# Host layout by tiles, merged weight halves and a reordered first stage in a two-branch mixer kernel

## The chip, the core and the metric

The kernel runs on one core of a Trainium2 chip. Five engines work side by side, each through its own queue in order: TensorE (PE; its weight loads are listed as PEld), VectorE (DVE), ScalarE (ACT), GpSimd (POOL) and SyncE (SP), which here issues all DMAs. The metric is the device time of one execution in microseconds (us). A profile shows one execution: its span runs from the first to the last instruction, and the time of that execution is a little longer than its span.

## The reference

One sequence of 2048 tokens with 512 channels. Each token is normalised, and the result goes two ways: a sliding, dilated attention with 32 heads of 16 channels, in which a token looks at itself and at 7 earlier ones at a distance of 2, 4, ... 14; and a two-layer MLP with 1376 hidden units. The branches are multiplied and added to the input.

```python
xn = _layernorm(x, axis=-1)
s = _A_ref(xn, A_wqkv, A_wo)            # attention, see below
g = _silu(_B_ref(xn, B_w1, B_b1, B_w2, B_b2))   # w2 . gelu(w1 . xn + b1) + b2
return x + s * g

# in _A_ref: H = 32, Dh = 16, W, dil = 8, 2
idx = pos[:, None] - off[None, :]       # off = arange(W) * dil, masked where negative
logits = einsum("bhsd,bhswd->bhsw", q, kg) * scale
o = einsum("bhsw,bhswd->bhsd", softmax(logits), vg)
return o.transpose(...).reshape(B, S, D) @ wo
```

## The kernel before

**Tiling.** Token s is p * 16 + i * 2 + c, with p the partition (0 to 127), i one of 8 tiles and c one of 2 parities. With a dilation of 2 the parities never meet in the attention, so the work is cut by c. A tile (c, i) is 128 tokens by 512 channels, 256 KB.

**Numbers in two halves.** Matmuls run in 16 bit. Every weight and every activation is split into a high half (rounded) and a low half (the rest), and a product is three matmuls: high by high, high by low, low by high. Weights are first scaled by a power of two that comes from the sum of their squares: ACT squares and sums (`sumsq`, L339; `prep_q`, L402), PE adds the sums over the partitions with a matrix of fours (`total`, L345), DVE takes the exponent and builds the scales in some four one-column operations (L349 to L369). Then `split` makes the high half on ACT (L376) and the low half on DVE (L377). The q, k and v weights have their own copy of this (L413 and L417).

**Stages.** For parity 0, `ln0` takes groups of tiles: statistics on DVE (L458, L459), the power -1/2 on POOL (L443), the normalised tile on DVE (L484) or ACT (L462), a transpose on PE (L491), high half on ACT (L495), low half on DVE (L496). Group order is tiles 2, 3, (0, 1), (4, 5), (6, 7). The loads ahead of it are the weights of head block 0 in two halves, then tiles 2, 3, (0, 1), (4, 5), (6, 7); behind them w1, head block 1, the rest of w1, w2 (L876 to L908). For parity 1, `ln1` does the same later through transposing DMAs.

The attention has 8 units (c, hb), a parity by a block of 8 heads. `qkv` is 8 tiles of 12 matmuls on PE (L545), and ACT scales them into one of two buffers U (L553); DMAs copy shifted rows for the neighbours (L562). `attention` is nearly all DVE: products with the eight neighbours (L596), sums over 16 channels (L599), softmax, products with the values (L653) and their sum (L648), the two halves of the result (L636 on ACT, L638 on DVE) and a transposing DMA to oT (L641).

The MLP is 44 steps (ch, f): 4 chunks of 512 tokens by 11 blocks of hidden units. `mlp1` does 12 matmuls of 512 columns (L785), gelu on ACT (L798), the high half on ACT (L801), the low half on DVE (L804), or, for the first 8 steps, on PE and ACT (L810, L813). `mlp2` adds the step into 4 PSUM tiles (L826), two steps behind `mlp1`. `mlp1` has two PSUM buffers (`mh`). The output projection is L723 (`wo_first` for parity 0, `wo_last` for parity 1), followed by a multiplication with the gate (L737, L767), the addition of x (L714, L716) and the store (L717).

**Order.** Nothing is ordered by hand. Each operation is registered with an engine, a duration, what it reads and writes and a priority (`Plan.add`); `Plan.issue` simulates the engines, at each step places the operation that can start first (within 0.05 us the one with the lowest priority number), and so fixes the order of every engine's queue. On the chip only the order remains: an operation that is ready still stands behind the one that was placed before it. Important priorities: statistics of `ln0` 0.1, evacuation of `qkv` 0.15, low halves of head block 0 0.135, head block 1 0.7, the sums of w2 0.74, w1 0.75, splits of w2 0.9; attention and `qkv` of later units 1000 and up, the MLP 1000000 and up.

Ring buffers (`Ring`) are given out in the same simulation: `prod` 3 of 8 KB a partition, `f` 7 of 2 KB, `ps` and `mh` 2 PSUM banks each.

Of the kernel before, what the change touches and what calls it, by code (L numbers as in the profile page):

```python
# [8 lines left out]
F32 = mybir.dt.float32  # L9
# [9 lines left out]
P = 128  # L19
# [12 lines left out]
NFB = 7  # L32
LAG = 2
# [4 lines left out]
LOADS = ["q0", (2, 1), (3, 1), (0, 2), (4, 2), (6, 2)]  # L38

ACT_Y = (0, 1, 4, 5)  # L40

# [29 lines left out]
class Plan:  # L71
# [5 lines left out]
    def __init__(self):  # L77
        self.ops, self.writer, self.readers, self.prio = [], {}, {}, 0.0

    def add(self, eng, dur, fn, reads=(), writes=(), prio=None, table=None, nbytes=0,  # L80
# [3 lines left out]

        o = Op()
# [24 lines left out]
        return o  # L110

# [25 lines left out]
    def place(self, o, t):  # L137

        if o.eng == "sp":
            if not o.nbytes:  # L140
                return t
            self.free["sp"] = t + o.issue
            self.dma = max(self.dma, t + o.issue + 0.3) + o.nbytes / o.rate
            end = self.dma + o.tail
            self.landed.append(end)
            return end
# [24 lines left out]
    def issue(self):  # L171
# [6 lines left out]
        while len(order) < len(self.ops):  # L178
            best = None
            for e, cand in engs.items():  # L180
# [13 lines left out]
                if lst:  # L194
                    t0 = min(x[0] for x in lst)
                    t, o = min((x for x in lst if x[0] <= t0 + WINDOW), key=lambda x: (x[1].prio, x[1].n))
                    if best is None or t < best[0]:
                        best = (t, o)
# [26 lines left out]

QUEUE = 8
# [6 lines left out]

PLN = 0.1
WINDOW = 0.05
DVE1 = 1.0417e-3
ACT1 = 0.833e-3


@with_exitstack  # L240
def tile_mixer(ctx, tc, a_x, a_wqkv, a_wo, b_w1, b_b1, b_w2, out):
# [30 lines left out]
    xv = a_x[0].rearrange("(p i c) d -> c p i d", i=NI, c=DIL)  # L272
    ov = out[0].rearrange("(p i c) d -> c p i d", i=NI, c=DIL)
    w1v = b_w1.rearrange("(k p) f -> p k f", p=P)


# [17 lines left out]
    wq = sb.tile([P, NHB, KT, 2, 384], F16, name="wq")  # L294
    w1 = sb.tile([P, KT, 2, F], F16, name="w1")
    w2 = sb.tile([P, NF, 2, D], F16, name="w2")
    wo = sb.tile([P, KT, 2, D], F16, name="wo")
# [6 lines left out]
    gd = dr.tile([DIL, P, NI, D], F32, name="gd")  # L304
# [30 lines left out]
    def sumsq(col, ckey, src, skey, junk, jkey):  # L335

        get = src if callable(src) else lambda: src
        n = get_n(src)
        act(n, lambda: nc.scalar.activation(junk().bitcast(BF16), get(), AF.Square, accum_out=col()),  # L339
            [skey], [ckey, jkey])  # L340

    def total(dst, dkey, cols, n, ckeys, late=False):

        b = (R_ps if late else R_z[0]).new()
        pl.add("pe", 0.3, lambda: nc.tensor.matmul(b.t[:, 0:n], fours, cols()[:, 0:n], start=True,  # L345
                                                   stop=True), ckeys, [b], prio=min(pl.prio, PTOT))
# [26 lines left out]
    def split(hi, lo, src, s, r, w):  # L373
        get = src if callable(src) else lambda: src
        n = get_n(src)
        act(n, lambda: nc.scalar.activation(hi, get(), AF.Identity, scale=s), r, [(w, "hi")])  # L376
# [11 lines left out]


    def load_q(hb):  # L390
        pre = pl.users(stkey[hb])
        for k in range(0, KT, 2):
            dma(P * 3072, lambda k=k: nc.sync.dma_start(stq[hb]()[:, k * 384:(k + 2) * 384],
                                                        a_wqkv[hb, :, k * 384:(k + 2) * 384]),
                [], [("stq", hb, k), ("stq", hb, k + 1)] + stkey[hb], after=pre)

    def prep_q(hb):
        col = R_s.new()
        for k in range(0, KT, 2):
            def go(k=k):  # L400
                src = stq[hb]()[:, k * 384:(k + 2) * 384]
                nc.scalar.activation(wq[:, hb, k:k + 2, 0].bitcast(BF16),  # L402
# [4 lines left out]
        total(lambda: ssq[:, hb:hb + 1], ("ssq", hb), lambda: col.t, 2, [(col, 0), (col, 2)],  # L407
              late=hb > 1)
        h = half_exp(lambda: ssq[:, hb:hb + 1], ("ssq", hb))
        up(qsc[:, hb, 0:1], ("qs", hb), h)  # L410
        for k in range(KT):
            def hi(k=k):
                nc.scalar.activation(wq[:, hb, k, 0], stq[hb]()[:, k * 384:(k + 1) * 384],  # L413
                                     AF.Identity, scale=qsc[:, hb, 0:1])

            def lo(k=k):
                nc.vector.scalar_tensor_tensor(  # L417
                    wq[:, hb, k, 1], stq[hb]()[:, k * 384:(k + 1) * 384], qsc[:, hb, 0:1],
                    wq[:, hb, k, 0], op0=ALU.mult, op1=ALU.subtract)
            r = [("stq", hb, k), ("qs", hb)]  # L420
            act(384, hi, r, [("wqh", hb, k)], holds=stkey[hb])
            dve(384, lo, r + [("wqh", hb, k)], [("wq", hb, k)], holds=stkey[hb], c=0.125,
                prio=0.135 if hb == 0 else None)
        down(qsc[:, hb, 1:2], ("qi", hb), h, 24.0)
# [5 lines left out]
    def factors(n, mv, mk, cdst, ckeys, **k):  # L430
# [11 lines left out]
            mk, [p0b], **k)  # L442
        pool(0.42 + 0.14 * n, lambda: nc.gpsimd.tensor_tensor(  # L443
            rb.t[:, 0:n], p0b.t[:, 0:n], halves[:, 0:n], op=ALU.pow), [p0b], [(rb, 0)], **k)
        dve(n, lambda: nc.vector.tensor_scalar(a0(), V(), EPS, None, op0=ALU.add), mk, [(A, 0)])
        dve(n, lambda: nc.vector.reciprocal(a1(), a0()), [(A, 0)], [(A, 1)])
        dve(n, lambda: nc.vector.tensor_tensor(a1(), a1(), V(), op=ALU.mult), [(A, 1)] + mk, [(A, 1)])
        dve(n, lambda: nc.vector.tensor_scalar(a1(), a1(), EPS, None, op0=ALU.add), [(A, 1)], [(A, 1)])
        dve(n, lambda: nc.vector.scalar_tensor_tensor(rb.t[:, 8:8 + n], mv()[:, 0:n, 0], -1.0,
                                                      rb.t[:, 0:n], op0=ALU.mult, op1=ALU.mult),  # L450
            mk + [(rb, 0)], [(rb, 1)], c=0.125, **k)
        pool(0.42 + 0.14 * n, lambda: nc.gpsimd.tensor_tensor(
            cdst, a1(), halves[:, 8:8 + n], op=ALU.pow), [(A, 1)], ckeys)
        return rb

    def stats(mv, a, key, x, xkey, **k):
# [9 lines left out]
    def ln0(ii, xs, xkeys):  # L466
# [5 lines left out]
        for a in range(n):  # L472
            stats(mv, a, mk[a], xs[a], xkeys[a], **first)
# [633 lines left out]
```

## Time and profile before

| | us |
|---|---|
| median of 3 runs | 425.3 (423.86 to 426.49) |
| the profiled execution: time | 426.52 |
| the profiled execution: span | 424.7 |
| time outside the span | 1.8 |
| granted TensorE clock, mean | 0.992 |

The page gives busy time by engine, the span in 40 slices as digits, the chain of work that ended last, and groups of instructions with count, busy time, mean duration in ns of one, and the engine's idle time before them. A line of the timeline is start, duration, engine, source line, operation, output <- inputs, and in brackets the idle time before it and what ended it; successive alike instructions are merged with a count. DVE's and ACT's instructions overlap a little, so that the mean duration is about 0.1 us over the step from one start to the next.

### The profile page before, as it was taken

To read this page: it belongs to the slowest core of one execution; us is meant where nothing else is said; L and a number is where in the kernel's file an instruction comes from. 1 tells how busy PE (TensorE), PEld (TensorE's weight loads), DVE (VectorE), ACT (ScalarE), POOL (GpSimd) and SP (SyncE) were. 2 spreads that over 40 slices of the span, in tenths; PEclk is the share of its full clock that TensorE was granted. 3 is DMA by queue.
4 is the path that set the end of the run, shared out by engine and by line. 5 is a ranking of instruction groups with operands and counts; after the bars stand their busy time and mean duration, and the time that the engine had idled before them with its cause. 6 is when DMAs were issued, how large, how long until landed. Compare 5 with 4: busy or idle time off the path is not lost.

```text
span 424.7 us, 5503 instructions
## 1 busy us (share of the span) xinstructions
PE 406.7 (96%) x2072; PEld 206.6 (49%) x2072; DVE 396.7 (93%) x434; ACT 217.6 (51%) x340; POOL 97.8 (23%) x87
## 2 busy tenths in 40 slices
PE   0999979999999999999999999999999999999995
PEld 0666524445544654445544654455445544444442
DVE  3998999998999979999999999998999999999966
ACT  4799975845376456744466254125312284226400
POOL 5310202002500382002700360046002610250013
PEclk9999969999999999999999999999999999999999
DMA  8964420003241235742162034022423264005325
GB/s 277 412 245 148 146 79 0 2 7 143 85 101 50 100 87 120 129 109 43 54 180 100 0 88 99 2 74 80 155 98 107 69 161 174 0 2 127 122 49 198
DMA packets 43050, 44.83 MB, mean 106 GB/s; under 512 B 27496, under 2 KB 28064, under 8 KB 42768
## 3 DMA queue, kind: packets, MB, share of 16 engines
q1 hardware_dynamic: 43024, 44.49, 34.7%
q8 instruction: 16, 0.26, 0.3%
q14 instruction: 10, 0.08, 0.1%
HBM read 23.53 MB, written 7.34 MB: 73 GB/s over the span
## 4 chain that ended last, share of the span: by engine, by line
PE 84%; ACT 9%; DVE 3%; DMA 2%; issue 1%; SPq 0%; DVEq 0%
PE z L826 27%; PE mh L785 26%; PE ps L545 22%; PE ps L723 6%; ACT w L376 2%; ACT U L553 2%; DMA prod<-in_A_x_dram 2%; ACT w L339 1%; PE z L723 1%; PE mh L723 1%; DVE U L714 1%; DVE U L767 1%; ACT wq L402 1%; ACT yT L495 1%; DVE bn L458 1%
## 5 line engine op out<-in xcount | busy, mean ns | idle before, releaser
L545 PE MATMUL ps<-wq,yT 128*128 128x384 f16 x768 | 129.3, 328 | 0.0
L785 PE MATMUL mh<-yT,w 128*128 128x512 f16 (+1 forms) x528 | 123.5, 385 | 0.9 <-ACT h L813 0.9
L826 PE MATMUL z<-w,h 128*128 128x512 f16 x480 | 112.0, 379 | 0.0
L545 PEld LDWEIGHTS <-yT 128*128 128x128 f16 x768 | 75.5, 99 | 51.1 <-issue 1.5
L785 PEld LDWEIGHTS <-w 128*128 128x128 f16 (+1 forms) x528 | 53.4, 101 | 65.8 <-issue 6.3
L798 ACT ACTIVATE mh<-mh,b1T,hsc 128x512 f32<-128x512 f32 (+1 forms) x44 | 33.0, 749 | 88.0 <-PE mh L785 87.8
L596 DVE TENSOR_TENSOR prod<-U 128x2048 f32<-128x2048 f32 x32 | 74.1, 2317 | 1.0
L826 PEld LDWEIGHTS <-h 128*128 128x128 f16 x480 | 47.1, 98 | 55.3 <-issue 0.3
L599 DVE TENSOR_REDUCE L<-prod 128x128 f32<-128x2048 f32 x32 | 72.9, 2279 | 0.3
L553 ACT ACTIVATE U<-ps,cs 128x384 f32<-128x384 f32 x64 | 37.2, 581 | 67.4 <-PE ps L545 63.4
L653 DVE TENSOR_TENSOR prod<-L,U 128x2048 f32<-128x2048 f32 x28 | 63.4, 2285 | 0.1
L676 POOL COPY gate<-prod 1x1 f32<-1x1 f32 x21 | 4.4, 208 | 210.7 <-DVE prod L596 204.2
L648 DVE TENSOR_TENSOR prod<-prod,prod 128x2048 f32<-128x2048 f32 x16 | 36.5, 2284 | 0.0
L677 POOL TENSOR_TENSOR prod<-prod 128x1024 f32<-128x1024 f32 x14 | 32.9, 2347 | 0.0
L723 PEld LDWEIGHTS <-oT 128*128 128x128 f16 x192 | 18.8, 98 | 22.4
L801 ACT ACTIVATE h<-mh,hsc 128x512 f16<-128x512 f32 x40 | 27.4, 685 | 0.9
L723 PE MATMUL ps<-wo,oT 128*128 128x512 f16 x120 | 26.9, 379 | 0.0
L804 DVE SCALAR_TENSOR_TENSOR h<-mh,hsc,h 128x512 f16<-128x512 f32 x32 | 23.8, 744 | 2.8 <-ACT h L801 2.8
L607 POOL TENSOR_TENSOR L<-L,misc 1x384 f32<-1x384 f32 x8 | 19.4, 2430 | 20.6 <-DVE L L599 20.6
L677 POOL TENSOR_TENSOR prod<-prod,prod 128x1024 f32<-128x1024 f32 x7 | 16.4, 2344 | 0.0
L798 ACT ACT_TABLE_LOAD x12 | 15.4, 1283 | 0.2
L636 ACT ACTIVATE o<-prod,osc 128x1024 f16<-128x1024 f32 (+1 forms) x9 | 9.4, 1050 | 11.5 <-DVE prod L648 6.2
(144 smaller groups left out, 338.1 us busy)
## 6 DMA issues: line engine op xcount, KB each, us to landing
f<-in_A_x_dram SPq DMA_DIRECT2D x31, 256.0 KB, 3.7
U<-U SPq DMA_DIRECT2D x16, 392.0 KB, 3.7
gd<-f SPq DMA_DIRECT2D x12, 256.0 KB, 2.0
oT<-in_B_w_dram SPq DMA_DIRECT2D x2, 1024.0 KB
yT<-in_B_w_dram SPq DMA_DIRECT2D x2, 1024.0 KB
f<-gd SPq DMA_DIRECT2D x8, 256.0 KB, 3.4
out_dram<-f SPq DMA_DIRECT2D x8, 256.0 KB, 2.0
out_dram<-U SPq DMA_DIRECT2D x8, 256.0 KB, 2.3
```

Of the source, the lines that this page charges most:

```text
L545: nc.tensor.matmul(b.t[:, 0:384], y[:, s, k, o:o + P], wq[:, hb, k, t], start=(n == 0), stop=(n == 11))
L553: act(384, lambda i=i, b=b: nc.scalar.activation(U3[:, i:i + 31:15, :], b.t[:, 0:384].rearrange("p (t e) -> p t e", t=3), AF.Identity, sca ...
L596: dve(2048, lambda p2=p2, g=g: nc.vector.tensor_tensor(p2(), q, slots(Ut, KH, 2 * g), op=ALU.mult), qk + [("kh", ub, 0), ("kh", ub, 1), (" ...
L599: dve(2048, lambda pr=pr, g=g: nc.vector.tensor_reduce(L3()[:, 2 * g:2 * g + 2], pr.t.rearrange("p (r f d) -> p r f d", r=2, d=DH), AX.X, ...
L648: dve(n, lambda: nc.vector.tensor_tensor(d(), a(), b(), op=ALU.add), keys, [dkey])
L653: dve(2048, lambda: nc.vector.tensor_tensor(pr.t.rearrange("p (r f d) -> p r f d", r=2, d=DH), L3()[:, 2 * g:2 * g + 2].rearrange("p r (f ...
L677: nc.gpsimd.tensor_tensor(x.t[:, 0:1024], x.t[:, 0:1024], y(), op=ALU.add)
L723: nc.tensor.matmul(b.t, oT[:, hb, i // 4, s, i % 4], wo[:, hb, t], start=(hb == 0 and n == 0), stop=(hb == NHB - 1 and n == 2))
L785: nc.tensor.matmul(b.t[0:M], w1[:, k, s, f * P:f * P + M], yT[ch][:, t, k], start=(n == 0), stop=(n == 11))
L798: act(512, lambda: nc.scalar.activation(b.t[0:M], b.t[0:M], AF.Gelu_apprx_tanh, bias=b1T[0:M, f:f + 1], scale=hsc[0:M, 1:2]), [b, ("b1T",) ...
L801: act(512, lambda: nc.scalar.activation(hi()[0:M], b.t[0:M], AF.Identity, scale=hsc[0:M, 2:3]), [b], [hk])
L826: nc.tensor.matmul(z.t, hl[s][0:K, t * P:(t + 1) * P], w2[0:K, f, w], start=(f == 0 and n == 0), stop=(f == NF - 1 and n == 2))
```

## The change

On the host x, the result, w1 and the buffer for the gate get new layouts: x and the result as (c, i, p, d), so that a tile is one piece of 256 KB in DRAM and not 128 rows 32 KB apart; w1 as [128, 4 * 1376], so that a part of any width is one run a partition. In the kernel:

- *Merged tensors.* The high halves of wq, w1, w2 and wo each become one block, the low halves another (`[P, 2, KT, F]` for `[P, KT, 2, F]`), so that one instruction can cross rows of weights. w1 is loaded, summed and split in 4 parts of 2048, 2048, 1024 and 384 columns instead of 8 (1024 and 352); w2 and wo in blocks of 1024 columns, head blocks 1 to 3 in blocks of 768.
- *Other engines.* w1's high halves go from ACT to DVE (`W1DVE`). The sums for w2's first eight rows go from DVE statistics (L974 to L981) to two ACT square sums of 2048 columns. The bias of ACT's normalisation is a one-column operation on ACT and no longer one on DVE behind POOL (L449).
- *Order.* Head block 0's weights and the first two x tiles are loaded in turn. Statistics of the pairs of tiles wait until tiles 2 and 3 are normalised (`behind`). Chains of small DVE operations are registered as one (`Plan.fuse`). The low halves of head block 0 get priority 0.45. w1's sums get 0.72, ahead of w2's, and wait for ACT's four normalised tiles (`BEFORE_W1`). The splits of w2 from row 4 on are put among the MLP's steps (`W2LATE`). A gelu of one element loads the table ahead of the first real one (`warm`). 16 matmuls whose result is not used, with the lowest priority, wait for the normalised tile 2 (`WAKE`). The tile order of the first unit is 2, 3, 0, 1, 4, ... The first matmuls of `qkv` and `mlp1` are registered in smaller groups.
- *Planner.* DMAs of the first 7.8 us are planned at 265 GB/s, those of the first loads otherwise at 395 to 400 GB/s with a shorter tail; ties between engines go by priority.

```diff
+W1C = [0, 2048, 4096, 5120, KT * F]
-LOADS = ["q0", (2, 1), (3, 1), (0, 2), (4, 2), (6, 2)]
+LOADS = ["q0", (2, 1), "q2", (3, 1), (0, 2), (4, 2), (6, 2)]
+W1DVE = (0, 1, 2, 3)
+W2P = (0, 2, 4, 6, 8, 9, 10)
+W2LATE = 4
+BEFORE_W1 = (0, 1, 4, 5)
...
+    def fuse(self, eng="dve"):
+        u = self.fused = dict(eng=eng, dur=0.0, fns=[], reads=[], writes=[], port=False, prio=1e12)
+        yield
+        self.fused = None
+        self.add(eng, u["dur"], lambda: [f() for f in u["fns"]], u["reads"], u["writes"],
+                 prio=u["prio"], port=u["port"])
...
-    xv = a_x[0].rearrange("(p i c) d -> c p i d", i=NI, c=DIL)
-    ov = out[0].rearrange("(p i c) d -> c p i d", i=NI, c=DIL)
+    xv, ov = a_x, out
...
-    w1 = sb.tile([P, KT, 2, F], F16, name="w1")
-    w2 = sb.tile([P, NF, 2, D], F16, name="w2")
+    w1 = sb.tile([P, 2, KT, F], F16, name="w1")
+    w2 = sb.tile([P, 2, NF, D], F16, name="w2")
...
+    def split(hi, lo, src, s, r, w, eng="act", n=None):
+        elif eng == "dve":
+            dve(n, lambda: nc.vector.tensor_scalar(hi, get(), s, None, op0=ALU.mult), r, [(w, "hi")], f=0.72)
...
+        behind = [("yd", i) for i in (2, 3) if n > 1]
+        fz = pl.fuse()
+        for a in range(n - 1):
+            stats(mv, a, mk[a], xs[a], [xkeys[a]] + behind)
+        fz.__enter__()
+        stats(mv, n - 1, mk[n - 1], xs[n - 1], [xkeys[n - 1]] + behind)
...
-    IORD = [2, 3, 1, 4, 5, 6, 7, 0]
+    IORD, IORD0 = [2, 3, 1, 4, 5, 6, 7, 0], [2, 3, 0, 1, 4, 5, 6, 7]
...
+    idle = fours.bitcast(BF16)
+    for _ in range(WAKE):
+        b = R_mh.new()
+        pl.add("pe", 0.2, lambda b=b: nc.tensor.matmul(b.t[:, 0:2 * P], idle[:, 0:P], idle, start=True,
+                                                       stop=True), [("yd", 2)], [b], prio=1e9)
...
+    for n in range(4):
+        with prio(PS1):
+            sumsq(lambda n=n: cw1.t[:, n:n + 1], (cw1, n), s1[n], [s1k[n]] + [("y_", i) for i in BEFORE_W1],
+                  lambda n=n: w1f[0][:, W1C[n]:W1C[n + 1]], ("w1h", n), W1C[n + 1] - W1C[n])
...
-            dve(512, lambda h=h, k=k, st=st: nc.vector.bn_stats(
-                st.t[:, 6 * k:6 * k + 6], (s2a, s2b)[h][:, k]), [("s2", h)], [(st, k)], port=False)
+        sumsq(lambda h=h: col5.t[:, h:h + 1], (col5, h), (s2a, s2b)[h].rearrange("p k f -> p (k f)"),
+              [("s2", h), (col5, h)], lambda h=h: w2[:, 0, 4 * h:4 * h + 4].rearrange("p k f -> p (k f)"),
+              ("w2j", h), 2048)
...
+        with prio(PW2 if k < W2LATE else PR_H + 1 + (10 * k - 15) * 1e-6):
+            split(*hl, src, zsc[0:K, 0:1], r, ("w2", k), "pool" if k in W2POOL else "act", n=512 * n)
+    act(1, lambda: nc.scalar.activation(warm, ident[0:1, 0:1], AF.Gelu_apprx_tanh),
+        [("y", 0, i) for i in range(NI)] + [("wq", 1, k) for k in range(KT)], [("warm",)], table="gelu")
...
+    lay["A_x"] = inputs["A_x"].reshape(P, NI, DIL, D).transpose(2, 1, 0, 3)
+    lay["B_w1"] = inputs["B_w1"].reshape(KT, P, F).transpose(1, 0, 2).reshape(P, KT * F)
```

340 lines of the change are left out of this document (188 added, 152 removed).

## The prediction

> **What bounds the kernel now.** I read the page first (busy shares, the clock row, the chain that ended last), then the waits of PE, then the timeline of the first 70 us, then the groups of instructions, then the last 30 us.
>
> ```profile
> span 424.7 us, 5503 instructions
> PE 406.7 (96%) x2072; PEld 206.6 (49%) x2072; DVE 396.7 (93%) x434; ACT 217.6 (51%) x340; POOL 97.8 (23%) x87
> PEclk9999969999999999999999999999999999999999
> PE 84%; ACT 9%; DVE 3%; DMA 2%; issue 1%; SPq 0%; DVEq 0%
> ```
>
> TensorE is busy nearly all the time, VectorE almost as much. The question is therefore where PE does not work at its pace, and how close behind it DVE is. The stretches from 60 to 400 us, summed, answer for the main part:
>
> ```profile
> sum 340.00, PE 340.00 PEld 169.60 DVE 329.10 ACT 164.06 POOL 79.34; mean PE 10.00 PEld 4.99 DVE 9.68 ACT 4.83 POOL 2.33
> ```
>
> PE never stops there, and DVE stops for only 11 us. So the change can win only before 60 us, in the clock dip that the clock row shows in its sixth slice, and in the last few us. PE's own waits are all early:
>
> ```profile
> PE z L345 <- ACT wq L402: 6.3, 1, 6.3
> PE z L491 <- DVE f L484: 4.3, 1, 4.3
> PE mh L810 <- ACT h L801: 2.1, 1, 2.1
> PE mh L785 <- ACT h L813: 0.9, 1, 0.9
> ```
>
> **The start: loads, first tile, first matmuls.**
>
> ```profile
> 9.27 1.29 DVE bn L458 x2
> ```
> ```profile
> 3.94 0.84 ACT L402 ACTIVATE wq<-prod 128x768 bf16<-128x768 f32 x1 [1.94 <-DMA prod<-in_A_wqkv_dram]
> 5.31 0.84 ACT L402 ACTIVATE wq<-prod 128x768 bf16<-128x768 f32 x1 [0.43 <-DMA prod<-in_A_wqkv_dram]
> 5.96 0.70 DVE L458 BATCH_NORM_STATS2 bn<-prod 128x6 f32<-128x512 f32 x1 [4.96 <-DMA prod<-in_A_x_dram]
> 7.90 1.09 POOL L443 TENSOR_TENSOR lw<-lw,halves 128x1 f32<-128x1 f32 x2 [2.96 <-DVE ssq L351]
> 8.38 2.13 ACT L413 ACTIVATE wq<-prod,qsc 128x384 f16<-128x384 f32 x4 [2.13 <-DVE qsc L369]
> 10.53 0.54 DVE L484 TENSOR_SCALAR f<-prod,lw,lw 128x512 f32<-128x512 f32 x1
> 11.22 1.94 PE L491 MATMUL z<-ident,f 128*128 128x128 f32 x8 [4.33 <-DVE f L484]
> 12.98 3.39 PE L545 MATMUL ps<-wq,yT 128*128 128x384 f16 x12
> 17.08 4.06 PE L545 MATMUL ps<-wq,yT 128*128 128x384 f16 x24
> ```
> ```profile
> L440 DVE TENSOR_SCALAR lw<-lw 128x2 f32<-128x2 f32 (+1 forms) x5 | 0.8, 158 | 0.0
> ```
>
> The first normalised tile (10.53) had its power from POOL at 7.90 + 1.09 = 8.99; it stood in DVE's queue behind the statistics of tiles 0 and 1, whose load landed only at 9.27. The change makes those statistics wait for the first two normalised tiles instead, and puts tile 2's load between the two weight halves. That half landed 0.65 us ahead of tile 2 (5.31, 5.96) and 1.37 behind the first (3.94): in turn, I put tile 2 at about 4.85 (3.94 plus 0.65 to 1.2) and the second weight half at 5.96. From there: statistics 0.70, about 0.4 for the three small operations behind them (0.158 each by the last row, now together and overlapping), POOL 0.55 (half of 1.09), so DVE normalises at about 6.6 and PE transposes at 7.2, 4.0 earlier than 11.22. From transposes to first matmuls took 12.98 - 11.22 = 1.76, giving 9.0. The weights come 0.65 later but their four scale operations no longer share DVE's queue with statistics, so the first high half is there near 8.6 and the last, at 2.13/4 each, at 10.2. First matmuls 9.0 to 9.5: 3.5 to 4.0 earlier.
>
> Not all of that lasts. Twelve matmuls took 3.39 at 12.98; 24 took 4.06 at 17.08, so 0.169 each when fast and 0.28 when slow. PE is at a slow pace from 11.22 to about 16.4, 5.2 us, though the clock row shows no dip there. The 16 idle matmuls wait for the same normalised tile as the first transposes, so they cannot begin the waking earlier; they only fill gaps. Waking at 7.2 + 5.2 = 12.4, the matmuls from 9.2 on lose about (12.4 - 9.2)/2 = 1.6, as much as now (3.39 - 12 x 0.169 = 1.4): no gain. By the slow 384-column matmul an idle one of 256 columns costs 0.28 x 256/384, at most 0.2; if all 16 stood ahead of needed ones they would cost 3.2, at the least nothing, since PE has about 1 us of gap behind the first transposes and more until the low weight halves exist. The low halves now have lower priority than all statistics; a PE gap of 0 to 2.5 us is the other unknown. I take 1 us for both together: 3.7 - 1.0 = 2.7 earlier when PE ends the first two head blocks.
>
> The Trainium skill ("TensorE: Matmul & The Clock Gate", What's actually happening) says the full clock comes after about 3.4 us of sustained work and not after a number of matmuls. The trace needed 5.2; by the page's figure the sum would be 0.9 us better, estimated. It speaks against the idle matmuls as such, which the trace bears out: they start no earlier than the work.
>
> **The middle: weights of the MLP, first gelu, clock dip.**
>
> ```profile
> 36.75 0.28 PE L345 MATMUL z<-s,fours 128*128 128x8 f32 x2
> 48.78 5.34 PE L785 MATMUL mh<-yT,w 128*128 128x512 f16 x24
> 56.23 0.38 PE L810 MATMUL mh<-h,dg 128*128 128x512 f16 x1 [2.10 <-ACT h L801]
> 57.47 5.28 PE L785 MATMUL mh<-yT,w 128*128 128x512 f16 x12 [0.87 <-ACT h L813]
> 66.24 2.75 PE L785 MATMUL mh<-yT,w 128*128 128x512 f16 x12
> ```
> ```profile
> 52.70 1.28 ACT L798 ACT_TABLE_LOAD   x1
> 54.00 0.75 ACT L798 ACTIVATE mh<-mh,b1T,hsc 128x512 f32<-128x512 f32 x1
> ```
> ```profile
> L376 ACT ACTIVATE w<-yT,zsc 128x512 f16<-128x512 f32 x8 | 5.3, 722 | 0.0
> L376 ACT ACTIVATE w<-oT,hsc 128x1024 f16<-128x1024 f32 x4 | 4.5, 1153 | 0.0
> L339 ACT ACTIVATE w<-oT 128x1024 bf16<-128x1024 f32 x4 | 4.2, 1058 | 0.0
> L339 ACT ACTIVATE w<-o 128x352 bf16<-128x352 f32 x2 | 1.0, 490 | 0.0
> L339 ACT ACTIVATION_READ_ACCUMULATOR w<-oT 128x1 f32 x4 | 0.8, 203 | 0.0
> L377 DVE SCALAR_TENSOR_TENSOR w<-yT,zsc,w 128x512 f16<-128x512 f32 x8 | 5.8, 744 | 0.0
> L377 DVE SCALAR_TENSOR_TENSOR w<-oT,hsc,w 128x1024 f16<-128x1024 f32 x4 | 4.9, 1274 | 0.0
> L596 DVE TENSOR_TENSOR prod<-U 128x2048 f32<-128x2048 f32 x32 | 74.1, 2317 | 1.0
> L974 DVE BATCH_NORM_STATS2 mx<-yT 128x6 f32<-128x512 f32 x8 | 5.3, 679 | 0.0
> L484 DVE TENSOR_SCALAR f<-prod,lw,lw 128x512 f32<-128x512 f32 x4 | 2.1, 542 | 0.0
> ```
>
> The first MLP block ends at about 48.78 + 2.67 = 51.4, but its gelu starts at 54.00, because ACT is still at weights and then loads a table. PE, with both buffers full, idles, and its next 12 matmuls run at half pace: 5.28 against 2.75 at 66.24, 2.5 us. If ACT is free in time, the correction matmul follows the second block at 48.78 + 5.19 = 53.97 and the third block starts 57.47 - 56.23 = 1.24 later, at 55.2 instead of 57.47: 2.3. With the dip gone, 2.3 + 2.5 = 4.8 us. PE then still idles about 0.9, against 2.1 + 0.9 now, which I take as too short for a dip.
>
> Is ACT free? Against now, ahead of the first gelu: high halves of w1 leave for DVE, 4 x 1.153 and four of 352 columns at the slope of these rows, (1153 - 722)/512 = 0.842 ns a column, so 0.59 each, -7.0; of w2's high halves eight of 0.722 and three of the same width become two of 1.153, the rest comes later, -7.9 + 2.3 (later ACT has room: 164 of 340 us); the w2 sums arrive, two of 2048 columns. A square sum costs (1058 - 490)/672 = 0.845 ns a column plus 0.19, and 0.20 to read it, so 2.13 each, +4.3; eight w1 sums become four, -1.6; a bias operation for four tiles, by the 0.203 row +0.8. In all -9.1. The table load only moves. ACT must be free at 51.4 - 2.7 = 48.7, 5.3 before 54.00: 3.8 us of margin, which also covers the idle time that ACT may get.
>
> Is w1 there? Its four sums now come ahead of w2's, so the total moves from 36.75 to about 32 to 33. Then DVE does high and low halves: high, 5504 columns at (542 - 158)/510 = 0.753 ns plus 4 x 0.158, 4.8 (542 for 512 columns, 158 for 2); low, 5504 at (1274 - 744)/512 = 1.035 ns plus 4 x 0.214, 6.6. That ends near 44.5, at 47 if one product of the attention (2.317) is put in between; PE needs three parts from 46.1 to 48. Tight, but in time. The high halves' bounds: 5504/512 x 0.542 = 5.8 above, the slope alone, 4.1, below; I keep 4.8, since both rows carry it.
>
> So PE arrives 2.7 + 4.8 = 7.5 us earlier: a span of 417.2 if it alone decides.
>
> **DVE and the end.**
>
> ```profile
> 407.93 0.75 DVE L638 SCALAR_TENSOR_TENSOR o<-prod,osc,o 128x512 f16<-128x512 f32 x1 [0.79 <-ACT o L636]
> 420.33 0.75 DVE L767 SCALAR_TENSOR_TENSOR U<-z,osc,U 128x512 f32<-128x512 f32 x1 [1.27 <-PE z L723]
> ```
> ```profile
> DMA to landing us min/median/max: 4.3/4.4/4.4
> ```
>
> The last attention output leaves DVE at 408.68; its transposing DMA lands 4.4 us later (413.1), and 12 matmuls (2.6) and the tail from 420.33 to 424.7 (4.4) remain: 420.1. PE hides that today. Once PE is over 4.6 us earlier, DVE sets the end. DVE's work changes by -5.3 (w2 statistics) and their small followers of about 1, -16 x 0.214 = -3.4 for sixteen merged low halves, +4.8: -4.9. But part of what goes lay ahead of the attention, where DVE may now stand idle until the first head block is complete, and late low halves of w2 move behind the start of the attention. Ends for DVE's gain: 0 and 5.7; I take 3, for the first head block is complete about 3 us earlier. 420.1 - 3 = 417.1, level with PE's 417.2.
>
> Forecast: span 417.2, 7.5 less. The profiled run took 426.52 (1.8 outside its span), 1.2 over the median 425.3; so 425.3 - 7.5 = 417.8. The new layouts of x, output and gate buffer move the same bytes in the same 2 KB rows; only the last store is on the path, so I count nothing for them beyond the order of the first loads.
>
> **The rivals.**
> - DVE gains nothing (idle where the statistics were): span 420.1, time about 420.7. For it: DVE stops only 11 us in 340. Against: it begins attention earlier. 0.14.
> - The middle stall stays: w1 arrives after PE, or ACT after it, so the dip returns. Only 2.7 remains: 422.0, time 422.6. For it: the 1 to 2 us of margin on w1. 0.12.
> - Better: PE keeps all 3.7 of the start; the idle matmuls close the gaps so that the cold loss (1.4) and the 0.9 us idle go too; and tiles laid out in one piece load faster. Today three tiles landed in 9.27 - 5.96 = 3.3 us, 1.1 each, against 0.65 for tile 2; at 0.65 the pair comes 1.4 sooner. 3.7 + 1.4 + 0.9 + 4.8 + 1.4 = 12.2: span 412.5, time 413.1. It needs 7.6 from DVE as well, more than its work shrinks, so half of its 11 us of stops would have to go. 0.18.
> - Slower: DVE takes over. The attention begins no earlier, and the high halves (4.8) and the late low halves of w2 (two of 1.274, three of 0.744: 4.8) all come on top of it: 420.1 + 9.6 = 429.7, time 430. It decides once DVE carries over 4.6 us more behind its first product than now. Against it: the low halves are done ahead today too. 0.06.
>
> **How the numbers follow.** The forecast has 0.50, with its own range 415 to 420. Low 412.5 takes in the better case, high 423 the stall at 422.6; only the slower rival and the far ends stay out. About 1 per cent (4.3 us) can be told from no change, so faster means under 421.0: 0.50 + 0.18 + two thirds of the DVE case 0.10 + a little of the stall 0.02: 0.80. Within: the rest of these two, 0.14, less 0.01 for a stall that grows: 0.13. Slower: 0.06 + 0.01 = 0.07.
>
> **What would show it.** First matmuls with wq near 9 to 9.5; a gelu near 49 with its table loaded before; no sixth-slice dip in the clock row; PE's waits after 20 us under 2 us; in the last 15 us a wait of PE for the last transposing DMA. Wrong if PE waits for w1 near 46, or if DVE's last attention output is not before 408.

## The result and the profile after

The changed kernel takes 428.06 us (median of 8, 427.61 to 430.1), the kernel before 424.47 on the same chip (median of 8, 423.81 to 426.49): a ratio of 1.0081, 95% interval 1.0063 to 1.01. It is slower by 0.8 per cent; 417.8 was predicted, in a range up to 423. The profiled execution took 430.1 (span 428.3), 2.0 above its median, as that of before stood 2.0 above its own (426.52 against 424.47), so the two traces may be set against each other: 3.6 us. (Both were taken in executions with a dip of the clock, which not every execution has; see the section on why the prediction was wrong.)

The page: span, busy shares, the granted clock, the chain that ended last.

```profile
span 428.3 us, 5505 instructions
PE 409.2 (96%) x2098; PEld 208.4 (49%) x2098; DVE 397.6 (93%) x400; ACT 218.7 (51%) x327; POOL 95.8 (22%) x87
PEclk9999989999999999999999999999999999999999
PE 69%; DVE 18%; ACT 4%; issue 3%; DMA 3%; SPq 1%; POOL 0%; DVEq 0%; ACTq 0%
```

DVE's share of the last chain went from 3 to 18 per cent. Its busy time did not fall. The dip in the clock stands at the sixth digit as before, only flatter (8 for 6): the granted clock is 0.50 between 58.0 and 61.2 us, and in the kernel before between 56.6 and 63.2.

**The start.** The timeline of the changed kernel, rows of DVE, PE and ACT:

```profile
6.39 0.55 DVE L559 TENSOR_SCALAR f<-prod,lw,lw 128x512 f32<-128x512 f32 x1
6.99 1.12 PE L566 MATMUL z<-ident,f 128*128 128x128 f32 x4 [1.49 <-DVE f L559]
10.06 0.37 PE L620 MATMUL ps<-wq,yT 128*128 128x384 f16 x1
...
14.69 0.81 ACT L532 ACTIVATE f<-prod,lw 128x512 f32<-128x512 f32 x1
...
18.89 0.68 DVE L523 BATCH_NORM_STATS2 bn<-prod 128x6 f32<-128x512 f32 x1
...
21.20 0.81 ACT L532 ACTIVATE f<-prod,lw 128x512 f32<-128x512 f32 x1
...
49.97 5.34 PE L862 MATMUL mh<-yT,w 128*128 128x512 f16 x24
```

The first tile is normalised 4.1 us earlier (10.53 before), the first matmuls with weights come 2.9 earlier (12.98). But the first tile on ACT is no earlier (14.69; 14.60 before), the statistics of tile 5 come at 18.89, and the next tile on ACT at 21.20 (19.99 before). The first MLP block starts at 49.97 instead of 48.78: the start loses 1.2 us.

**The middle.** First the first split of w2 in the timeline of the kernel before, then the timeline of the changed kernel, with the way of w2's sums to its scale:

```profile
36.50 0.72 ACT L376 ACTIVATE w<-yT,zsc 128x512 f16<-128x512 f32 x1
```
```profile
43.94 0.21 ACT L1068 ACTIVATION_READ_ACCUMULATOR w<-f 97x1 f32 x1
...
44.83 1.28 ACT L1098 ACT_TABLE_LOAD   x1
...
47.24 0.28 PE L394 MATMUL z<-s,fours 128*128 128x5 f32 x2
...
49.72 0.14 DVE L418 TENSOR_SCALAR zsc<-s 128x1 int32<-128x1 int32 x1
...
49.90 1.15 ACT L434 ACTIVATE w<-yT,zsc 128x1024 f16<-128x1024 f32 x1 [1.09 <-DVE zsc L418]
...
51.41 2.18 ACT L434 ACTIVATE w<-yT,zsc 128x1024 f16<-128x1024 f32 x2
53.49 0.74 ACT L879 ACTIVATE mh<-mh,b1T,hsc 128x512 f32<-128x512 f32 x1
54.16 1.14 ACT L434 ACTIVATE w<-yT,zsc 128x1024 f16<-128x1024 f32 x1
55.20 0.68 ACT L882 ACTIVATE h<-mh,hsc 128x512 f16<-128x512 f32 x1
...
57.78 2.60 PE L862 MATMUL mh<-yT,w 128*128 128x512 f16 x6 [1.48 <-ACT h L894]
```

The table is loaded early, as intended. But the last of w2's sums is there only at 44.15, PE adds them up at 47.24, DVE has the scale at 49.86, and ACT, which has waited for it, starts the splits at 49.9, 13.4 us later than before. From there they stand ahead of the first gelu (53.49; 54.00 before) and between it and its high half (55.20). PE's third MLP block starts at 57.78 (57.47 before).

**DVE.** Two windows, before and then after: busy time of PE, PEld, DVE, ACT and POOL.

```profile
25.00:40.00 15.00, 15.00 (x97) 9.27 (x96) 13.88 (x39) 15.00 (x39) 0.38 (x1) 1.00 0.50 162
```
```profile
25.00:40.00 15.00, 14.77 (x95) 9.29 (x96) 7.83 (x20) 15.00 (x26) 0.00 (x0) 1.00 0.42 120
```

DVE, busy 13.88 of these 15 us before, is busy 7.83: what stood there, w2's statistics, is gone, and nothing else is ready. Its first product of the attention comes at 57.54 (37.98 and 56.97 before). The timeline, at PE's one wait after 60 us and in the last us, behind the first row of the last projection in the kernel before:

```profile
411.06 1.46 PE L723 MATMUL ps<-wo,oT 128*128 128x512 f16 x6
```
```profile
229.31 2.75 PE L862 MATMUL mh<-yT,w 128*128 128x512 f16 x12 [1.87 <-DVE h L885]
...
411.93 0.75 DVE L713 SCALAR_TENSOR_TENSOR o<-prod,osc,o 128x512 f16<-128x512 f32 x1 [0.79 <-ACT o L711]
...
414.68 1.46 PE L798 MATMUL ps<-wo,oT 128*128 128x512 f16 x6
...
415.52 1.41 DVE L842 SCALAR_TENSOR_TENSOR U<-ps,osc,U 128x512 f32<-128x512 f32 x2 [2.84 <-PE ps L798]
...
417.27 4.70 PE L798 MATMUL z<-wo,oT 128*128 128x512 f16 x21
423.36 1.20 DVE L789 TENSOR_TENSOR U<-U 128x512 f32<-128x512 f32 x1
```

DVE leaves its last attention output at 412.68, 4.0 later than before, and PE has to wait for it once on the way (229.31), where it never stopped before. PE's last matmul ends at 421.97 (420.29 before: 413.65 + 6.64), and 6.3 us follow it instead of 4.4: the tail is now DVE's chain from 415.52 to 424.56, without a stop. 1.7 + 1.9 are the 3.6 us.

Both parts can be followed further. Up to 225 us PE had started 563 matmuls of the MLP, against 561 before; up to 231 us, behind its wait, 581 against 589. At 0.217 us each (12 take 2.6) it was 0.4 us ahead and is 1.7 behind from there to the end, so the 1.7 come with that one wait. The 1.9 are a matter of order. From the first six matmuls of the last projection (411.06 before, 414.68 after) to the end it is 13.6 us in both kernels; but from these six on only 33 of the projections' 192 matmuls are left, where the planner had left 42, and nine more ahead of them take 2.0 us.

### The profile page after: what moved, and what is told of

Read it like the earlier page. It is cut to its first block, busy times and chain, and to the rows that moved or that the text cites. A ratio compares the mean times of both kernels' runs of the same rounds, so it can differ in the third digit from the quotient of the medians.

```text
span 428.3 us, 5505 instructions
## 1 busy us (share of the span) xinstructions
PE 409.2 (96%) x2098; PEld 208.4 (49%) x2098; DVE 397.6 (93%) x400; ACT 218.7 (51%) x327; POOL 95.8 (22%) x87
## 4 chain that ended last, share of the span: by engine, by line
PE 69%; DVE 18%; ACT 4%; issue 3%; DMA 3%; SPq 1%; POOL 0%; DVEq 0%; ACTq 0%
PE z L907 21%; PE mh L862 20%; PE ps L620 19%; PE ps L798 6%; DVE L L674 3%; DVE prod L671 2%; DMA f<-in_A_x_dram 2%; DVE prod L728 1%; DVE w L435 1%; PE z L798 1%; DMA prod<-in_A_x_dram 1%; ACT w L434 1%; DVE prod L723 1%; DVE h L885 1%; PE mh L798 1%
## 5 line engine op out<-in xcount | busy, mean ns | idle before, releaser
L671 DVE TENSOR_TENSOR prod<-U 128x2048 f32<-128x2048 f32 x32 | 75.0, 2347 | 2.2 <-DMA U<-U 1.1
L752 POOL TENSOR_TENSOR prod<-prod,prod 128x1024 f32<-128x1024 f32 x7 | 16.4, 2342 | 0.0
```

The source lines that it names most:

```text
L671: dve(2048, lambda p2=p2, g=g: nc.vector.tensor_tensor(p2(), q, slots(Ut, KH, 2 * g), op=ALU.mult), qk + [("kh", ub, 0), ("kh", ub, 1), (" ...
L752: nc.gpsimd.tensor_tensor(x.t[:, 0:1024], x.t[:, 0:1024], y(), op=ALU.add)
```

## The experiments

The theories, as named in the expectations. T1: w1's sums are held back, so w1's scale is late and DVE has its hole. T2: the tiles starve PE from 10 to 28 us. T3: w2's scale is late, so its splits collide with the first gelus. T4: chains of small DVE operations, registered as one, cost time in that start. Beside each time stands its ratio to the kernel before in the same set of runs; "fourth gelu" is a mark for how far the MLP has come (68.14 after, 69.03 before).

**w1's sums set free.**

```diff
-BEFORE_W1 = (0, 1, 4, 5)
+BEFORE_W1 = ()
```

> The changed kernel with one edit: w1's square sums no longer wait for ACT's four normalised tiles. T1 (w1's scale is late because its sums are held back, so DVE stands idle from 25 to 40 us and all splits come ahead of the first attention product): the first two sums go back into ACT's idle time between 10 and 20 us, w1's total on PE moves from 37.8 to 32-34, DVE is busy 10 us or more between 25 and 40 (7.83 in the changed kernel), its last attention output ends near 410.5 (412.7), time 426 +-0.7. T2 (the starved tiles between 10 and 25 us cost the time): nothing is won, or up to 1 us is lost because a sum delays a tile; 428-429. T3 (w2's late splits between the gelus): 428.

428.11 us, 1.0049 (1.0035 to 1.0062). The total of w1 came at 34.27, and DVE was busy 9.39 of the 15 us. w2's first split came at 43.64 instead of 49.90 and the third block without its wait, the fourth gelu at 66.60; but the first MLP block started 0.8 later (50.80), and PE waited 1.96 for DVE at 227.78. Some 1.4 us better in the ratio, not by T1's road. Nor does T3 cover what is left: w2's scale is early here, PE does not wait for a gelu, and the kernel is still slower than the one before.

**w2's statistics back on DVE.**

```diff
-        sumsq(lambda h=h: col5.t[:, h:h + 1], (col5, h), (s2a, s2b)[h]...
+            dve(512, lambda h=h, k=k, st=st: nc.vector.bn_stats(
+                st.t[:, 6 * k:6 * k + 6], (s2a, s2b)[h][:, k]), [("s2", h)], [(st, k)], port=False)
...
```

> The changed kernel with one edit: the sums of w2's first eight rows are DVE statistics again, as in the kernel before. T1: they fill the hole of DVE (25 to 40: 12-13 busy instead of 7.83) and ACT has 4 us less to do ahead of w2's scale, which comes from 49.8 to about 46; w1's scale stays near 38, so the attention still begins late; DVE's last output 411-412, time 426.5-427.5. T2: 428. T3 (w2's scale is late, so that its splits collide with the gelus): w2's scale comes 3-4 us sooner, the first gelu near 51 instead of 53.5, third block near 56, time 426.

424.87 us, 0.9983 (0.997 to 0.9997): the whole loss is gone, and the kernel before is just beaten. Its timeline:

```profile
45.32 2.19 ACT L434 ACTIVATE w<-yT,zsc 128x1024 f16<-128x1024 f32 x2 [0.34 <-DVE zsc L413]
...
52.84 0.75 ACT L879 ACTIVATE mh<-mh,b1T,hsc 128x512 f32<-128x512 f32 x1
53.62 0.69 ACT L882 ACTIVATE h<-mh,hsc 128x512 f16<-128x512 f32 x1
...
54.79 3.04 PE L862 MATMUL mh<-yT,w 128*128 128x512 f16 x12
...
408.46 0.75 DVE L713 SCALAR_TENSOR_TENSOR o<-prod,osc,o 128x512 f16<-128x512 f32 x1 [0.79 <-ACT o L711]
```

The splits are through before the first gelu, its high half follows at once, PE has no wait for a gelu, and the fourth gelu comes at 64.72, 4.3 before that of the kernel before. DVE has 6 us more to do than in the changed kernel (403.9 against 397.6 busy) and is done with the attention 3.5 sooner (409.21). T3 expected 426 and T1 426.5 to 427.5; it is better than both.

**Both together.**

```diff
-BEFORE_W1 = (0, 1, 4, 5)
+BEFORE_W1 = ()
-        sumsq(lambda h=h: col5.t[:, h:h + 1], (col5, h), (s2a, s2b)[h]...
+            dve(512, lambda h=h, k=k, st=st: nc.vector.bn_stats(...
```

> Both edits of the two kernels before this one together. T1: w1's scale near 34 and nothing of w2 in the way; DVE busy 13 or more between 25 and 40, first attention product before 50 instead of 57.5, last output at or before 409, time 424-425, so the 3.6 us are back and the start's gain shows only at PE. T2: 428. T3: between 426 and 427, from w2's scale alone.

427.95 us, 1.0059 (1.0036 to 1.0083). w1's total at 34.07, DVE busy 13.61, no hole: but the first product still came at 55.70, and the time is 3 us worse than without the freed sums. The fourth gelu came at 65.74, and PE waited 1.82 for DVE at 226.76. T1 falls: an early w1 buys nothing. But w2's first split came at 42.35, earlier than with the statistics alone (45.32), so a late scale of w2 is not needed for a loss of this size; where the wait of 1.82 comes from is read in the run with ACT's unused sums, below.

**The layouts alone**, in the kernel before (x, result and gate buffer by tiles, the order of the work unchanged).

```diff
-    xv = a_x[0].rearrange("(p i c) d -> c p i d", i=NI, c=DIL)
+    xv, ov = a_x, out
...
-    gd = dr.tile([DIL, P, NI, D], F32, name="gd")
+    gd = dr.tile([DIL, NI, P, D], F32, name="gd")
...
```

> The kernel before with only the new layouts of x, result and gate buffer, tile by tile in one piece; its order of work is as before. T1 and the prediction: same rows of 2 KB, so 424.5 +-1 (at most 1 us sooner from the pairs of tiles at the start). Rival: pieces of 256 KB in one place meet fewer DMA engines or memory banks at a time and land later; then 426-428 and the pair of tiles 0 and 1 lands after 9.27.

426.05 us, 1.0001 (0.9989 to 1.0014): nothing, as predicted. Its one profiled execution took 1535.67 us, with PE busy for 1518.5 of them, and can't be set beside the other traces; but in its start the statistics of tiles 0 and 1 begin at 8.96 without waiting for their load (9.27 before), so the rival's later landing is not seen.

**Four parts of the new start, each undone alone**, for T2 and T4: the chains, the wait of the pairs' statistics, the order of loads, the idle matmuls.

```diff
-        u = self.fused = dict(eng=eng, dur=0.0, fns=[], reads=[], writes=[], port=False, prio=1e12)
         yield
-        self.fused = None
-        self.add(eng, u["dur"], lambda: [f() for f in u["fns"]], u["reads"], u["writes"], ...
```

> The changed kernel with one edit: the small DVE operations of a chain are registered one by one again, so that others may stand between them. T4 (fused chains starve PE between 10 and 28 us: a chained operation takes 0.19 us from start to start against 0.07 where another stands between, and the statistics of tile 5, fused with its chain, came at 18.9 though its load had landed): tiles 4 and 5 are normalised before 20 us instead of 21.2 and 22.2, PE's first MLP block starts near 48.5 instead of 49.97. Rival (the tiles wait for loads or for POOL): 49.5 to 50.5. The time itself also hangs on the order that the planner makes of the rest: 424 to 428.

```diff
-        behind = [("yd", i) for i in (2, 3) if n > 1]
+        behind = []
```

> The changed kernel with one edit: the statistics of the pairs of tiles don't wait for the first two normalised tiles. If that wait starves PE: tiles 0 and 1 get their statistics at 9-10 instead of 10.9 and 12.4, are normalised near 13 instead of 14.7 and 15.7, tile 3 some 1.2 us later than now (11 instead of 9.8), and the first MLP block starts 0.5 to 1.5 us before 49.97. If the chains behind the statistics set the pace: within 0.3 us of 49.97.

```diff
-LOADS = ["q0", (2, 1), "q2", (3, 1), (0, 2), (4, 2), (6, 2)]
+LOADS = ["q0", "q2", (2, 1), (3, 1), (0, 2), (4, 2), (6, 2)]
```

> The changed kernel with one edit: both weight halves are loaded ahead of the first two tiles, as in the kernel before. If the early tile is worth something where it counts: first transposes near 8.5-9 instead of 7.0, first matmuls with weights near 10.5-11 instead of 10.06, first MLP block 1 us or more later than 49.97. If the later tiles set the pace (my theory): the first matmuls move, the first MLP block stays within 0.4 us of 49.97, and the time within 1 us of 428.5 unless the order of the rest changes.

```diff
-WAKE = 16
+WAKE = 0
```

> The changed kernel without the 16 idle matmuls. If they only fill gaps: first MLP block within 0.3 us of 49.97 and the time within 0.7 of 428.5. If they keep TensorE fast between the tiles: the 384-column matmuls between 10 and 16 us run at 0.28 us instead of 0.17, and everything behind is 0.5 to 1.5 us later. If they stand in the way of needed work: up to 1 us sooner.

| undone | us | ratio | first MLP block at | first and third tile on ACT at |
|---|---|---|---|---|
| none | 428.06 | 1.0081 (1.0063 to 1.01) | 49.97 | 14.69, 21.20 |
| chains | 429.93 | 1.0105 (1.0077 to 1.0132) | 50.76 | 17.11, 20.31 |
| wait of the pairs | 428.05 | 1.008 (1.0056 to 1.0103) | 51.18 | 15.90, 22.41 |
| loads in turn | 430.4 | 1.0119 (1.0094 to 1.0145) | 51.83 | 17.66, 22.46 |
| idle matmuls | 429.04 | 1.0088 (1.0064 to 1.0113) | 50.04 | 14.76, 21.28 |

Three of the four are worth 0.8 to 1.9 us at the first MLP block, where I had held it likelier that they are worth nothing or do harm: none is to blame for the late block. None of them is the culprit that T2 looks for, and the start's 1.2 us are not what the later runs won back. The idle matmuls are worth nothing. Chains bring the first pair of tiles sooner and the second later, so T4 is true of tiles 4 and 5 alone.

**ACT's load and DVE's hole parted.** DVE makes the statistics, ACT makes its two square sums as well, without use. (The edit is shown against the kernel with the statistics on DVE.)

```diff
+        sumsq(lambda h=h: col6.t[:, h:h + 1], (col6, h), (s2a, s2b)[h].rearrange("p k f -> p (k f)"),
+              [("s2", h)], lambda h=h: w2[:, 0, 4 * h:4 * h + 4].rearrange("p k f -> p (k f)"),
+              ("w2j", h), 2048)
```

> As e2 (statistics of w2's first eight rows on DVE, and these make the scale), but ACT also makes the two square sums of 2048 columns that it makes in the changed kernel, at the same priority; their result is not used. This parts the two things that e2 changed. If e2's gain is ACT's relief ahead of the gelus: w2's high halves come 3-4 us later than in e2, PE waits for the first gelu again, third MLP block near 57 instead of 54.8, time 427-428. If it is the filled hole on DVE (work that is done in idle time instead of nowhere): DVE's last attention output stays within 1 us of e2's 409.2 and the time within 1 us of e2's.

428.0 us, 1.0068 (1.0048 to 1.0088). Its window and its timeline:

```profile
25.00:40.00 15.00, 14.77 (x95) 9.32 (x96) 13.33 (x34) 15.00 (x26) 0.00 (x0) 1.00 0.44 138
```
```profile
50.00 1.15 ACT L434 ACTIVATE w<-yT,zsc 128x1024 f16<-128x1024 f32 x1 [1.11 <-DVE zsc L418]
...
53.60 0.73 ACT L879 ACTIVATE mh<-mh,b1T,hsc 128x512 f32<-128x512 f32 x1
54.26 1.14 ACT L434 ACTIVATE w<-yT,zsc 128x1024 f16<-128x1024 f32 x1
...
57.88 1.46 PE L862 MATMUL mh<-yT,w 128*128 128x512 f16 x6 [1.48 <-ACT h L894]
...
227.18 2.75 PE L862 MATMUL mh<-yT,w 128*128 128x512 f16 x12 [1.33 <-DVE h L885]
```

The hole is filled (13.33), yet ACT's middle is the changed kernel's within 0.1 us, and so is the time: its interval overlaps the changed kernel's. The two square sums on ACT are the only edit that parts this kernel from the one with the statistics on DVE alone (424.87), and the planner's order follows from it: 0.85 per cent, or 3.6 us, as much as the change lost. DVE's last attention output (410.55) is 2.1 sooner than in the changed kernel; nothing of that can be told in the time.

By the two traces (spans 426.2 and 423.0, both without a dip of the clock) T3 holds for some 2.1 us: PE's waits for ACT at 56.02 (0.62) and at 57.88 (1.48), as in the changed kernel (0.61 and 1.48). The 1.33 at 227.18 are another matter. There PE waits for the low half of the MLP's 24th step, and this stands in DVE's queue behind two products of the attention, where with the statistics alone it stands behind one. This kernel first, then the one with the statistics alone:

```profile
221.97 4.49 DVE L728 TENSOR_TENSOR prod<-L,U 128x2048 f32<-128x2048 f32 x2
226.38 0.74 DVE L885 SCALAR_TENSOR_TENSOR h<-mh,hsc,h 128x512 f16<-128x512 f32 x1
```
```profile
221.33 2.29 DVE L728 TENSOR_TENSOR prod<-L,U 128x2048 f32<-128x2048 f32 x1
223.54 0.74 DVE L885 SCALAR_TENSOR_TENSOR h<-mh,hsc,h 128x512 f16<-128x512 f32 x1
```

DVE comes to the first product only 0.64 later, and behind one product the low half would have been done by 225, before PE stopped at 225.85 (an estimate from these rows): it is the planner's order and not a late DVE that makes this wait. The same low half stands behind two products in the changed kernel and in both kernels with freed sums, and PE waits 1.87, 1.96 and 1.82 us for it. No run changes this order alone: how much of the 3.6 us it would give back is not shown.

**w1's high halves to ACT**, all four parts, and the last two, both with the statistics on DVE.

```diff
-W1DVE = (0, 1, 2, 3)
+W1DVE = ()
```

> e2 with all of w1's high halves back on ACT. If DVE's work is what sets the end of e2 (its last attention output at 409.2, and 13.9 us of tail behind it): DVE has 3.6-3.7 us less to do, last output near 406, time 421-422, provided that ACT (7 us more ahead of the first gelu) is ready by 52; if ACT isn't, the first gelu comes near 55 instead of 52.8, TensorE's clock dips and the time is 425-427.

```diff
-W1DVE = (0, 1, 2, 3)
+W1DVE = (0, 1)
```

> e2 with the last two parts of w1's high halves (1024 and 384 columns) on ACT, the first two on DVE. DVE has 1.1 us less, ACT 1.8 us more ahead of the first gelu. If DVE sets the end and ACT has room: 423.5-424.5. If ACT is the limit in the middle: 425-426.

All four: 426.35 us, 1.0023 (1.0007 to 1.0038). The second case of the expectation came, though in the profiled execution the clock did not dip. DVE's last output came at 405.64, 3.6 sooner, and the tail of the timeline shows that it no longer sets the end, since DVE waits for PE:

```profile
404.89 0.75 DVE L713 SCALAR_TENSOR_TENSOR o<-prod,osc,o 128x512 f16<-128x512 f32 x1 [0.79 <-ACT o L711]
...
419.59 0.75 DVE L842 SCALAR_TENSOR_TENSOR U<-z,osc,U 128x512 f32<-128x512 f32 x1 [1.84 <-PE z L798]
```

But ACT was late again: the first gelu at 53.71, the third block at 57.55 behind a wait of 1.47. Two parts: 426.94 us, 1.0036 (1.0013 to 1.0059), against an expected 423.5 to 424.5. The middle was that of the statistics' run to 0.1 us, but PE waited 1.52 at 60.25 for sums of the next head block's weights, which the planner had put ahead of the MLP and which themselves waited 2.11 for their load. Six of its twelve executions had a lower mean clock (0.992 or 0.993) and took 427.46 to 428.26, the others 424.73 to 426.42. A miss that neither theory had.

**w2's splits all ahead of the MLP.**

```diff
-W2LATE = 4
+W2LATE = 99
```

> The changed kernel with one edit: the splits of w2 from row 4 on are not put among the MLP's steps. If the late place of these splits is to blame (two of ACT's splits stand between the first gelus at 54.2 and 55.8): the third MLP block comes before 57.78 and the time is 426-427. If the late scale of w2 (49.7) is to blame: all splits then stand ahead of the first gelu or of the second, which comes 2-4 us later; time 429-432.

430.44 us, 1.0124 (1.0104 to 1.0145); the first gelu came at 56.44. The late place of the splits is no fault; that the late scale is to blame was the case of the expectation that came.

**What sets the pace of the tiles.** With the statistics on DVE: first without the low halves of head block 0's weights, then with tiles 6 and 7 normalised on ACT.

```diff
-            dve(n, lambda src=src, dst=dst: nc.vector.scalar_tensor_tensor(
-                dst[1], src(), qsc[:, hb, 0:1], dst[0], op0=ALU.mult, op1=ALU.subtract),
...
+            if hb == 0 and k == 0:
+                pool(0.9, lambda: nc.gpsimd.memset(wq[:, 0, 1], 0.0), [], [("wq", 0, j) for j in range(KT)],
+                     prio=0.01)
+            if hb > 0:
...
```

> e2, but the low halves of head block 0's weights are left out of the computation: POOL sets them to zero at the start, so DVE has four operations of 0.6 us less between 11 and 18 us. If DVE's queue sets the pace of the tiles between 9 and 21 us: tiles 4 and 5 are normalised 1.5-2.4 us sooner than in e2 (21.3 and 22.4), and the first MLP block starts 1-2 us before e2's 50.05. If the loads, POOL or ACT set it: within 0.4 us of 50.05.

```diff
-ACT_Y = (0, 1, 4, 5)
+ACT_Y = (0, 1, 4, 5, 6)
```

> e2, with the last two tiles (6 and 7) normalised on ACT too, which stands idle a third of the time between 10 and 25 us; DVE has 1.1 us less. If DVE's queue is the pace: first MLP block 0.5-1 us before 50.05, time 424-424.5, provided the order of the rest stays as it is in e2. If not: 50.05 or later (ACT's 0.81 against DVE's 0.54 and a one-column operation more), time 425-426.

Without the low halves: 424.69 us, 0.9988 (0.9967 to 1.0009). From its timeline:

```profile
7.56 1.11 PE L569 MATMUL z<-ident,f 128*128 128x128 f32 x4 [1.94 <-DVE f L562]
...
18.69 0.81 ACT L535 ACTIVATE f<-prod,lw 128x512 f32<-128x512 f32 x1
...
24.89 2.11 PE L623 MATMUL ps<-wq,yT 128*128 128x384 f16 x12 [0.66 <-ACT U L631]
```

Tile 4 is normalised at 18.69 against 21.34: 2.65 us sooner for 2.4 us of DVE's work taken away. DVE's queue does set the pace of the tiles. The first MLP block moved only from 50.05 to 49.56, where 1 to 2 us were expected: POOL's clearing had delayed the first transposes by 0.64, and PE now waited for ACT to empty its buffers (0.66 at 24.89, 0.42 at 45.66). With tiles 6 and 7 on ACT: 429.7 us, 1.0089 (1.0066 to 1.0112), first block at 51.51; ACT's added operations made its other work late, a clear miss.

## Why the prediction was wrong

**The first failed step is in the middle**: "Is ACT free? ... In all -9.1 ... 3.8 us of margin". It added up ACT's work and never asked when ACT may begin the splits of w2. They need w2's scale; that needs all of w2's sums, then PE, which took them 3.1 us after the last was there, then DVE, which was at w1's low halves until 49.1. By moving two sums to ACT, behind w1's (held until 27.43), the change put the first split from 45.3 (the run with the statistics on DVE) to 49.9. ACT idled just before it and was late just after: PE waited 2.1 us for it at the first gelus, and not at all with the early scale. The sum of work may well have been right; the due time was not in it. Of the forecast 7.5 us PE had 0.4 at 225 us. What then put it behind the kernel before, the wait for DVE at 229.31 and the order of the last projection, came from the planner's new order, which no step of the prediction looked at.

Where the scale is early (the statistics on DVE), the fourth gelu comes 4.3 us before that of the kernel before although the first MLP block is 1.3 later, so 5.6 for the forecast 4.8. But this is against an execution with the full dip, and **the term for the dip, 2.5 us, was too large for the time it was taken from**. The runs of the kernel before that stand beside the run with ACT's unused sums show it: seven had a mean clock of 0.992 and took 425.95 to 427.03 (median 426.39), seven had 0.998 or 0.999 and took 423.51 to 425.15 (424.20). So the dip is worth 2.2 us, and a part of the executions does without it already. The forecast read it in the one profiled execution (426.52, clock 0.992) and took it in full from a median of 425.3, 1.2 below that execution. The change's loss does not hang on this: at a mean clock of 0.998 the changed kernel took 427.94 to 428.05.

**The start.** Its first steps hold: transposes at 6.99 (7.2 said), matmuls at 10.06 (9.0 to 9.5 said; the matmul over the sums stood behind the transposes on PE, 7.90, and the scale operations behind the small ones of tile 3 on DVE, 8.59). "3.7 - 1.0 = 2.7 earlier when PE ends the first two head blocks" failed: -1.2. It took PE's gaps at 0 to 2.5 us and carried the rest through. The tiles behind the first two come out of DVE's queue, which was full from 9 us on in both kernels and gave them no sooner. That this queue sets their pace is shown by the run without low halves; how the 1.2 is made up of chains, order and ACT is not settled.

**w1.** Its total came at 37.79, not at 32 to 33: the held sums were named in the text on the change and left out of the sum. It did no harm, for PE never waited for w1, with the sums held or freed. High halves took 3.6 us (4.8 said), low halves 6.8 (6.6).

**DVE.** Work of -4.9 was +0.9 in the page, gain of 3 was -4.0. Durations were added where starts count. Eight low halves of 512 columns last 0.744 each, but three of them in a row took 2.06 (0.66 from start to start); four of 1024 took 4.87 (1.20). So merging two saves 0.12, not 0.21, and a chain of dependent small operations gains no overlap at all. To 400 us DVE was busy 3.5 us less than before, so most of the 4.0 is idle time. The rival "DVE takes over" saw the attention begin no earlier, and priced it at 430, the nearest of the rivals to the 428.06; DVE did come 4.0 late, and PE waited for it at 229.31, but the run with ACT's unused sums says that its hole was not what cost the time.

**The end.** "4.4 ... and 12 matmuls (2.6) and the tail from 420.33 to 424.7 (4.4) remain: 420.1" left out that DVE has 9 us of its own in the tail. In three runs in which PE never waited for DVE (statistics on DVE, with two parts on ACT, without low halves) the span ends 13.8, 13.8 and 13.9 us behind DVE's last attention output. By that, an estimate, the kernel before would have ended at 408.68 + 13.8 = 422.5 without an earlier DVE, however early PE: 2.2 us of gain, not 4.6, and the forecast needed 5.3 us from DVE. PE did not stop in these three tails either, so they do not show that 13.8 is the least.

**What was right**: the layouts (nothing), the idle matmuls (they begin with the first tile and fill gaps), no wait for w1 near 46. What would show it wrong did: DVE's last output not before 408. Of the signs that would show it right, the gelu near 49 (53.49) and the clock row without a dip failed.

## What to carry to other kernels

When work is moved to an engine with room, add up not its hours but its dates: what waits for the result, what stands ahead of it in that queue, and how many other queues the result has still to cross. Idle time that a change leaves early in a busy engine is seen only in windows, for the busy share of the whole span (93 per cent both times) hides it; whether it costs anything takes a run in which it alone is filled, and here it cost nothing that could be told. Where a planner orders all queues anew after each edit, compare the orders too: one product more ahead of one operation, some 170 us behind the first effect of the edit, cost PE up to 2 us. A gain that is read in one execution must be there in the executions that make the median. And a first result that comes early is worth what the second and third do: follow the queue that feeds them.

## What the runs showed of the hardware

*Restarting the clock.* In the run without the pairs' wait PE had a gap of only 0.83 us at the start, and its matmuls stayed slow long after it:

```profile
8.19 2.08 PE L1006 MATMUL mh<-fours 128*128 128x256 bf16 x9
11.10 0.48 PE L620 MATMUL ps<-wq,yT 128*128 128x384 f16 x1 [0.83 <-ACT wq L481]
13.29 2.90 PE L620 MATMUL ps<-wq,yT 128*128 128x384 f16 x9
16.02 0.60 PE L1006 MATMUL mh<-fours 128*128 128x256 bf16 x4
```

Nine took 2.90 us; in the changed kernel, with no such gap, nine took 1.62 from 11.41 on, 4.4 us after the first transposes. After the gap it took to 16.02, 4.9 us from 11.10 and 9.0 from the first transposes (6.99): as if the waking had begun anew. One execution shows it, and that the gap is the reason was not tested. The clock row shows no dip there. The Trainium skill ("TensorE: Matmul & The Clock Gate", What's actually happening) gives 3.4 us of sustained work; these runs needed 4.4 to 5.2 (5.2 in the kernel before, 11.22 to 16.4).

*Small operations on DVE.* In the changed kernel, links of one chain that depend on each other start 0.18 to 0.21 us apart, each 0.15 to 0.17 long:

```profile
10.27 0.15 DVE L513 TENSOR_SCALAR lw<-lw 128x1 f32<-128x1 f32 x1
10.45 0.16 DVE L514 RECIPROCAL lw<-lw 128x1 f32<-128x1 f32 x1
10.65 0.16 DVE L515 TENSOR_TENSOR lw<-lw,lw 128x1 f32<-128x1 f32 x1
10.85 0.15 DVE L516 TENSOR_SCALAR lw<-lw 128x1 f32<-128x1 f32 x1
10.92 0.69 DVE L523 BATCH_NORM_STATS2 bn<-prod 128x6 f32<-128x512 f32 x1
```

An operation that does not depend on the one ahead of it starts 0.07 later (10.92 behind 10.85). Registering a chain as one gives up this overlap.
